# First four pairs' scores from float32 operands on two row halves, zero products at the start, one value block per pair, shared tail products, and an order from a table: a fused attention and gated MLP on one Trainium2 core

## The chip, the cores and the metric

The kernel runs on one core of a Trainium2 chip. The metric is the device time of one execution in microseconds (us), the median of several runs. An engine is named as the profile names it: PE is the matrix engine and PEld its weight loads, DVE the vector engine, ACT the scalar engine, POOL the GpSimd engine, and SP the engine whose queue issues all the DMA transfers of this kernel.

## The reference

For each of 8 batches and 8 heads, 576 queries of 64 numbers meet 576 keys. Scores further than tau below their row's maximum are dropped; the rest go through a softmax and weight the values. The 8 heads of a batch, side by side, are then the input of a gated MLP whose gate mixes along the sequence:

```python
scores = scale * np.matmul(q, k.transpose(0, 1, 3, 2))
thresh = np.max(scores, axis=-1, keepdims=True) - tau
scores = np.where(scores >= thresh, scores, -1000000000.0)
attn = np.exp(scores - np.max(scores, axis=-1, keepdims=True))
attn = attn / (np.sum(attn, axis=-1, keepdims=True) + 1e-09)
x = np.matmul(attn, v)                      # heads side by side: 576 x 512 per batch
h = gelu(x @ w_in)                          # 576 x 1024
u, v = h[..., :512], h[..., 512:]
v_n = layernorm(v) * g_ln
v_s = w_sg @ v_n + b_sg[:, None]            # along the sequence
out = x + (u * v_s) @ w_out
```

## The kernel before

**Pairs and tiles.** Work is cut into 32 *pairs*, two heads of one batch each (`attention(n, ...)`, n = 0 to 31), and 8 batches of the MLP (`moe(b, ...)`), each of which needs its four pairs. A head's 576 queries are four tiles of 128 and a tail of 64; the tails of the two heads share one tile, so a pair has 9 score tiles of 128 x 576. For each tile, PE makes the scores (`scores`, L750), DVE takes the row maximum (`maxima`, L759), POOL the threshold (L765), ACT the exponential (L785), DVE drops what lies below the threshold and sums (`select`, L792), PE transposes the tile in 128 x 128 pieces (`turn`, L516; 45 per pair with those of the inverse sums) and ACT copies the result out (L870, L889). Then PE multiplies by the values (`values`, L900), DVE multiplies by the inverse sums (`finish`, L912), and ACT and POOL split the result `x` into a high part `xh` and a rest `xl` (L916, L920).

**Split operands.** A product with full precision is made from operands that are split into a high part and a rest in the format fp32r: high times high, high times rest, rest times high, three products of one pass each. `products` (L980) issues those of the MLP. Plain float32 operands need no split, but the array takes several passes; the profile shows such a product as two records. For the scores of a pair, one operand `qst` stacks the high part and the rest of q over the 128 rows, `ks` holds the high part of k twice, and `klz` the rest of k beside zeros, so two products give a score half of 288 columns; the shared tail tile takes four. Placing q and k for this needs ACT (L665), POOL (L669, L692) and ten DMAs of a pair (L676, L684, L698). Only pair 0 (`WHOLE_SCORES = 1`) uses plain float32 operands `rk`, `rq` of 64 rows each, with no splitting and placing.

**Value blocks.** `values` is called twice per pair, for 256 and for 320 queries (`PARTS`), each a block of 10 products of plain float32, 64 columns of the array per head, two heads beside each other: 20 records.

**The MLP of a batch** has five v units (four of 128 rows, one of the 64 tail rows, 512 columns, 12 products each: L1037 to L1074 normalise them), then u, gate and down units (L1114, L1128, L1132, L1157, L1160). Its weights arrive as doubles and are turned into split float32 by `from_double`: 16 jobs, five steps on DVE each (L553 to L567), two on ACT (L547, L548) and the splitting (L568, L569).

**The order.** The kernel is first recorded by a `Planner`, which gives every step a place (`Step.time` plus an offset per kind, `OFF`, and per group, `START`), prices each operation (`time_of`), and lists the steps in the order in which its engines would take them: among the steps ready within `LOOK[engine]` of the soonest, the one with the lowest place. PE's eight banks are handed out in the same walk. The real program is then written in this one order, and each engine and the SP queue run their instructions in it, one after the other.

## Time and profile before

| | |
|---|---|
| times of the runs shown (us) | 1030.94, 1033.41, 1036.24; median 1033.41 |
| the profiled execution: span (us) | 1032.0, 1.4 below the median and within the runs |
| instructions in the trace | 20160 |
| mean granted clock of PE | 0.995 |

The profile's span runs from the first to the last instruction; the time of a run has been within 4.2 of it in all three. Views of the profile used below: the busy table by engine, the stretches (busy time and number of instructions of each engine between two times), the groups of instructions by line, the chain of work that ended last, the timeline, the waits, and the DMA issues. In a group's row, `x` is the count, then come the busy time and the mean of one in ns, then the engine's idle time just before them. In a row of the chain or the timeline the first number is the start, the second the length, both in us.

### The profile page before, as it was taken

What the parts mean: (1) busy time and instruction counts of PE and PEld (TensorE: products, weight loads), DVE (VectorE), ACT (ScalarE), POOL (GpSimd) and SP (SyncE); (2) the same over time, 40 slices, a digit from 0 to 9 for tenths busy, and PEclk for the clock granted to TensorE, in tenths of its full rate; (3) what the DMA queues carried; (4) which work ended last, traced back from release to release, by engine and by line L of the source; (5) the groups of instructions that cost most, each with busy time, mean ns of one, the idle gap of its engine ahead of it and who ended that gap; (6) DMA issues with size and microseconds to landing.
All of it is one profiled execution on the core that took longest, in us unless ns stands there. A gap on an engine that the chain in (4) does not pass through costs nothing.

```text
span 1032.0 us, 20160 instructions
## 1 busy us (share of the span) xinstructions
PE 985.4 (95%) x6972; PEld 839.1 (81%) x6972; DVE 664.5 (64%) x1431; ACT 696.3 (67%) x1501; POOL 606.4 (59%) x1085
## 2 busy tenths in 40 slices
PE   4988989999999999999999999999999999999997
PEld 2666767898779987799788988799878997889887
DVE  3888998573776647855586647766477564773350
ACT  4788788674786658856687657766578665875362
POOL 5575668655565475554656565554746646644566
PEclk9999999999999999999999999999999999999999
DMA  8575353343242434324143342424334242300001
GB/s 248 136 202 129 91 137 84 91 117 104 60 112 60 110 100 110 97 78 106 58 108 87 108 114 69 103 54 115 101 86 108 64 113 65 98 21 22 21 7 47
DMA packets 51336, 96.43 MB, mean 93 GB/s; under 512 B 8097, under 2 KB 16289, under 8 KB 51234
## 3 DMA queue, kind: packets, MB, share of 16 engines
q1 hardware_dynamic: 51234, 95.15, 34.7%
q8 instruction: 55, 0.90, 0.4%
q14 instruction: 47, 0.39, 0.1%
HBM read 38.44 MB, written 9.44 MB: 46 GB/s over the span
## 4 chain that ended last, share of the span: by engine, by line
PE 59%; DMA 10%; POOL 9%; ACT 8%; DVE 7%; issue 6%; SPq 1%; POOLq 0%; DVEq 0%; ACTq 0%
PE all_banks L980 26%; PE all_banks L750 12%; PE all_banks L900 11%; PE all_banks L516 10%; DMA qst<-qhi 4%; DVE p L792 3%; ACT pt L870 2%; POOL ot L1160 2%; DMA qst<-rq 2%; DMA ks<-khi 1%; ACT p L785 1%; DMA w<-in_w_in 1%; DVE nm L759 1%; POOL rk L669 1%; POOL vv L1059 1%
## 5 line engine op out<-in xcount | busy, mean ns | idle before, releaser
L792 DVE SCALAR_TENSOR_TENSOR p<-all_banks,nm,p 128x576 f32<-128x576 f32 x256 | 204.6, 812 | 96.3 <-ACT p L785 51.0
L759 DVE TENSOR_REDUCE nm<-all_banks 128x1 f32<-128x576 f32 x288 | 212.3, 751 | 69.4 <-PE all_banks L750 65.3
L785 ACT ACTIVATE p<-all_banks,nm 128x576 f32<-128x576 f32 x256 | 187.3, 747 | 51.1 <-DVE nm L759 49.3
L750 PE MATMUL all_banks<-ks,qst 128*128 128x288 f32 x620 | 186.6, 319 | 7.2 <-DVE p L792 3.5
L516 PE MATMUL all_banks<-ident_r,p 128*128 128x128 f32 x1152 | 168.2, 282 | 15.5 <-DVE p L792 12.9
L870 ACT ACTIVATE pt<-all_banks 128x512 f32<-128x512 f32 (+1 forms) x320 | 165.4, 556 | 13.6 <-PE all_banks L516 12.4
L750 PE MATMUL all_banks<-klz,qst 128*128 128x288 f32 x620 | 172.5, 296 | 0.2
L516 PEld LDWEIGHTS all_banks<-ident_r,p 128*128 128x128 f32 x1152 | 135.7, 145 | 37.8 <-DVE p L792 15.9
L750 PEld LDWEIGHTS all_banks<-ks,qst 128*128 128x128 f32 x620 | 117.7, 190 | 30.9 <-DVE p L792 14.6
L900 PE MATMUL all_banks<-pt,rv 128*64 128x320 f32 (+1 forms) x1024 | 138.3, 412 | 1.7 <-ACT ir L832 1.5
L750 PEld LDWEIGHTS all_banks<-klz,qst 128*128 128x128 f32 x620 | 118.0, 190 | 2.1 <-DMA klz<-rk 0.6
L765 POOL TENSOR_TENSOR nm<-columns,nm 128x1 f32<-128x1 f32 x288 | 57.7, 207 | 99.6 <-DVE nm L759 76.0
L980 PE MATMUL all_banks<-wsh,z 128*128 128x288 f32 (+2 forms) x512 | 112.7, 296 | 1.5 <-DVE uu L963 0.6
L900 PEld LDWEIGHTS all_banks<-pt,rv 128*64 128x64 f32 x1024 | 67.8, 136 | 50.9 <-issue 8.8
L980 PEld LDWEIGHTS all_banks<-wsh,z 128*128 128x128 f32 x512 | 85.4, 188 | 2.8 <-DVE uu L963 0.9
L1132 POOL TENSOR_TENSOR gl<-uu,gh 128x288 fp32r<-128x288 f32 (+2 forms) x64 | 51.3, 804 | 54.7 <-ACT gh L1128 54.6
L980 PE MATMUL all_banks<-xh,wih 128*128 128x288 f32 (+2 forms) x256 | 78.4, 306 | 0.0
L980 PE MATMUL all_banks<-xh,wil 128*128 128x288 f32 (+2 forms) x256 | 76.5, 299 | 0.0
L980 PE MATMUL all_banks<-gh,woh 128*128 128x288 f32 (+2 forms) x256 | 76.3, 299 | 0.1
L980 PE MATMUL all_banks<-gl,woh 128*128 128x288 f32 (+2 forms) x256 | 75.5, 296 | 0.6 <-POOL gl L1132 0.5
L980 PE MATMUL all_banks<-xl,wih 128*128 128x288 f32 (+2 forms) x256 | 75.4, 295 | 0.0
L980 PE MATMUL all_banks<-wsl,z 128*128 128x288 f32 (+2 forms) x256 | 75.4, 294 | 0.0
(114 smaller groups left out, 2192.7 us busy)
## 6 DMA issues: line engine op xcount, KB each, us to landing
rk<-in_kT SPq DMA_DIRECT2D x32, 320.0 KB, 3.2
rv<-in_vP SPq DMA_DIRECT2D x32, 320.0 KB, 3.1
ks<-khi SPq DMA_DIRECT2D x62, 160.0 KB, 2.6
rq<-in_qT SPq DMA_DIRECT2D x32, 288.0 KB, 3.1
qst<-rq SPq DMA_DIRECT2D x62, 144.0 KB, 3.1
qst<-qhi SPq DMA_DIRECT2D x62, 144.0 KB, 3.4
ks<-khi SPq DMA_DIRECT2D x62, 144.0 KB, 2.5
out_T<-ot SPq DMA_DIRECT2D x56, 144.0 KB, 1.8
```

Of the source, the lines that this page charges most:

```text
L516: nc.tensor.transpose(out, x, ident_r.bitcast(F32))
L669: nc.gpsimd.tensor_tensor(st["k"].bitcast(F32R), st["k"], st["kh"], ALU.subtract)
L750: nc.tensor.matmul(sc[:, a, 0:HALF], w, x, start=(j == 0), stop=(j == len(terms) - 1))
L759: nc.vector.tensor_reduce(nmax, st["s", h, i][:, :, 0:HALF], AX.XY, ALU.max, negate=True)
L765: nc.gpsimd.tensor_tensor(thr, toff, st["nm", h, i], ALU.subtract)
L785: nc.scalar.activation(target(h, i), st["s", h, i][:, :, 0:HALF], AF.Exp, bias=st["nm", h, i])
L792: nc.vector.scalar_tensor_tensor(dst, st["s", h, i][:, :, 0:HALF], st["thr", h, i], dst, ALU.is_ge, ALU.mult, accum_out=st["l", p][:, c:c ...
L870: nc.scalar.activation(dst, src, AF.Copy)
L900: nc.tensor.matmul(acc[h * D:(h + 1) * D, 0:w], st["v"][:, o:o + D], unit(h, p)[:, kt, 0:w] if kt < NM else tail_unit(p)[:, 0:w], start=(k ...
L980: nc.tensor.matmul(st["acc"], *term(j), start=(j == 0), stop=(j == n - 1))
L1132: nc.gpsimd.tensor_tensor(st["gl", p, d], st["u", p, d], st["gh", p, d], ALU.subtract)
L1160: return lambda: nc.gpsimd.tensor_tensor(o(), o(), x[b, m][:, ts_], ALU.add)
```

## The change

1. **Scores of pairs 0 to 3** come from float32 operands (`WHOLE_SCORES = 4`). `half_scores` issues one product per half and head, and the two heads' products, in the upper and the lower 64 rows of the array, follow each other. The shared tail tile is made on row halves and column halves at once. Pairs 0 to 3 need no splitting or placing of q and k, and their q and k are loaded at the start into eight separate places.
2. **Scores of pairs 4 to 31**: the rest of k (`kl`) is used where POOL writes it, against the high part of q beside zeros (`qz`, two DMAs per pair, one set for all pairs); the tail tile takes three products instead of four, with `qd`, a diagonal of the two tails (two small DMAs). `klz` and its DMAs are gone.
3. **One value block per pair** (40 records in two banks), and with it one guard, reciprocal, inverse, multiply and split per pair; the last pair keeps two.
4. **Shared tail products**: the tail of `xl` is also written behind `xh` (one POOL instruction per pair), so the v unit of the tail makes 8 products of 128 rows instead of 12 of 64; ACT copies the upper half out and DVE adds it.
5. **Zero products**: six float32 products of 256 columns on the zeroed `pm` are the first thing PE does. The zeroing of constants moves from POOL to DVE.
6. **Order**: each step's place comes from a table of numbers (packed in `PLACES`) in place of `OFF` and `START`; `LOOK` and the planner's prices are other numbers, and it counts a price of 165 ns where PE's products change between the whole array and halves of it.

```diff
-OFF = dict(
-    tau=18.0, q_tails=18.88, w_load=-20.35, w_abs=-36.92, w_word=1.51, w_mul=108.69, w_add=115.91, w_hi=-17.64,
...
+PLACES = (
+    "c-nPX2Rv2p|G($jWbctZvq!clg>2FiDMTd^iS)A)Q8biNW|7h&Eg~{Pp|UrTJ+jyB-gEx$IQO3G`})6J=id9A=RD76z2Berb5Rh4LT$WIge&0%"
...
-LOOK = dict(tensor=124.5, vector=56.7, scalar=75.9, gpsimd=57.5, sync=1079.7)
-WHOLE_SCORES = 1
+LOOK = dict(tensor=71.71, vector=187.35, scalar=179.86, gpsimd=257.13, sync=1209.65)
+WHOLE_SCORES = 4
+WARM = 6
...
-        self.place = [0.0] + [s.time + s.scale * OFF[s.kind] + START.get(s.group, 0.0) for s in plan]
+        table = np.frombuffer(zlib.decompress(base64.b85decode(PLACES)), np.uint8).astype(np.uint16).reshape(2, -1)
+        places = np.cumsum((table[0] * 256 + table[1]).astype(np.int16).astype(int))
...
+        def f(k):
+            x = bank(f"warm{k}")
+            nc.tensor.matmul(x[:, 0:2 * P], pm[:, 0:P], pm[:, 0:2 * P], start=True, stop=True)
...
+        parts = SPLIT if n == B * HP - 1 else ((0, S),)
...
-            nc.gpsimd.tensor_tensor(st["k"].bitcast(F32R), st["k"], st["kh"], ALU.subtract)
+            st["kl"] = kpool.tile([P, KW], F32R, tag="kl", name=f"kl{n}")
+            nc.gpsimd.tensor_tensor(st["kl"], st["k"], st["kh"], ALU.subtract)
...
-        def k_place_lo(h):
-            def f():
-                rows, (w, o) = slice(h * D, (h + 1) * D), (KW, 0) if h else (S, TAIL)
-                st["kl", h] = klz[h][n % 2]
-                nc.sync.dma_start(st["kl", h][rows].bitcast(F32), st["k"][rows, o:o + w])
-            return f
+        def q_place_alone():
+            for h in range(2):
+                rows = slice(h * D, (h + 1) * D)
+                nc.sync.dma_start(qz[h][rows].bitcast(F32), st["qh"][rows, :S].bitcast(F32))
...
+                rows, o, lo = slice(h * D, (h + 1) * D), i * P, a * HALF + (1 - h) * TAIL
+                qo = o + h * TAIL
+                nc.tensor.matmul(st["s", h, i][:, a, 0:HALF], st["q"][rows, qo:qo + P], st["k"][rows, lo:lo + HALF],
+                                 start=True, stop=True)
...
-                    elif i < NM:
-                        terms = [(q[h][:, qo:qo + P], k[:, ko:ko + HALF]) for k in (st["ks", h], st["kl", h])]
+                    if i < NM:
+                        terms = [(q[h][:, qo:qo + P], st["ks", h][:, ko:ko + HALF]),
+                                 (qz[h][:, qo - h * TAIL:qo - h * TAIL + P], st["kl"][:, lo:lo + HALF])]
                     else:
-                        terms = [(w, k[:, ko + g * TAIL:ko + g * TAIL + HALF])
-                                 for g, w in enumerate((q[0][:, MAIN:KW], q[1][:, 0:P]))
-                                 for k in (st["ks", g], st["kl", g])]
+                        terms = [(w, st["ks", g][:, ko + g * TAIL:ko + g * TAIL + HALF])
+                                 for g, w in enumerate((q[0][:, MAIN:KW], q[1][:, 0:P]))]
+                        terms.append((qd[n % 2], st["kl"][:, TAIL + ko:TAIL + ko + HALF]))
...
+                for a, (c0, w) in enumerate(got):
+                    for kt in range(NM + 1):
+                        for h in range(2):
+                            o, cs = kt * P + h * D, slice(c0, c0 + w)
+                            nc.tensor.matmul(st["acc", p][h * D:(h + 1) * D, a, 0:w], st["v"][:, o:o + D],
+                                             unit(h)[:, kt, cs] if kt < NM else tail_unit()[:, cs],
+                                             start=(kt == 0), stop=(kt == NM))
...
+                c, k = divmod(j, 2)
+                return xh_of[b, c][:, ts_], (wih, wil)[k][c][:, FH:DF]
...
-            acc = products(put, time, spread, f"v{b}_{i}", (rows, FH), term, 3 * NC)
+            acc = products(put, time, spread, f"v{b}_{i}", (P, FH), term, (3 if i < NM else 2) * NC)
...
+        for k in range(WARM):
+            at("warm", 0.0, partial(f, k))
```

What the table and the new code do to the order is seen at two places. The first is DVE around the multiply of pair 3 (`x32_3` before, `ir3` now), after which the products of batch 0 can begin; `w` and `room` are steps of the weight jobs, `nm` and `p` those of score tiles. Before:

```order
L963 SCALAR_TENSOR_TENSOR vv0_1_1274<-gt0_1_1231,all_banks_91 128x512
L559 TENSOR_SCALAR room6_807<-w6_744 128x512
L1037 BN_STATS bn0_1_1296<-vv0_1_1274 128x6
L792 SCALAR_TENSOR_TENSOR p4_0_1213,l4_0_1214<-all_banks_91,nm4_1_0_1251,p4_0_1213 128x576
L1040 BN_AGGR bn0_1_1296<-bn0_1_1296 128x2
L759 TENSOR_REDUCE nm4_1_1_1311<-all_banks_91 128x1
L792 SCALAR_TENSOR_TENSOR p4_1_1288,l4_0_1214<-all_banks_91,nm4_0_1_1266,p4_1_1288 128x576
L912 TENSOR_TENSOR x32_3_1_1331<-all_banks_91,ir3_1_1268 128x320
L792 SCALAR_TENSOR_TENSOR p4_1_1288,l4_0_1214<-all_banks_91,nm4_1_1_1311,p4_1_1288 128x576
L553 TENSOR_SCALAR room14_1318<-room14_1318 128x256
L555 TENSOR_SCALAR room7_832<-room7_832 128x512
```

And now:

```order
L668 TENSOR_TENSOR w18_944<-w18_944 128x256
L654 TENSOR_SCALAR room19_969<-room19_969 128x256
L656 TENSOR_SCALAR room19_969<-room19_969 128x256
L658 SCALAR_TENSOR_TENSOR w19_932<-w19_932,room19_969 128x256
L668 TENSOR_TENSOR w20_1037<-w20_1037 128x256
L902 SCALAR_TENSOR_TENSOR p4_0_1138,l4_1139<-all_banks_91,nm4_0_0_1133,p4_0_1138 128x576
L660 TENSOR_SCALAR room19_969<-w19_932 128x256
L1037 TENSOR_TENSOR ir3_1090<-all_banks_91,ir3_1090 128x576
L870 TENSOR_REDUCE nm4_1_0_1165<-all_banks_91 128x1
L668 TENSOR_TENSOR w19_932<-w19_932 128x256
L870 TENSOR_REDUCE nm4_0_1_1177<-all_banks_91 128x1
```

Before, 53 of the 80 DVE steps of the weight jobs stand ahead of this multiply, with some of pair 4 and two early v units of batch 0; now 79 of the 80 do, with one tile of pair 4 and nothing of the MLP.

The second place is PE in the v unit of the tail of batch 0 (`wih`, `wil` are the split halves of w_in, `xh`, `xl` those of x, by pair). Before, 12 products for 64 rows:

```order
L980 MATMUL all_banks_91<-wih0_104,xh0_470 64x512
L980 MATMUL all_banks_91<-wil0_108,xh0_470 64x512
L980 MATMUL all_banks_91<-wih0_104,xl0_484 64x512
L980 MATMUL all_banks_91<-wih1_105,xh1_646 64x512
L980 MATMUL all_banks_91<-wil1_109,xh1_646 64x512
L980 MATMUL all_banks_91<-wih1_105,xl1_673 64x512
L980 MATMUL all_banks_91<-wih2_106,xh2_938 64x512
L980 MATMUL all_banks_91<-wil2_110,xh2_938 64x512
L980 MATMUL all_banks_91<-wih2_106,xl2_983 64x512
L980 MATMUL all_banks_91<-wih3_107,xh3_1177 64x512
L980 MATMUL all_banks_91<-wil3_111,xh3_1177 64x512
L980 MATMUL all_banks_91<-wih3_107,xl3_1203 64x512
```

And now 8 for 128 rows, the row of the first one included:

```order
L1113 MATMUL all_banks_91<-wih0_104,xh0_475 128x512
L1113 MATMUL all_banks_91<-wil0_108,xh0_475 128x512
L1113 MATMUL all_banks_91<-wih1_105,xh1_705 128x512
L1113 MATMUL all_banks_91<-wil1_109,xh1_705 128x512
L1113 MATMUL all_banks_91<-wih2_106,xh2_946 128x512
L1113 MATMUL all_banks_91<-wil2_110,xh2_946 128x512
L1113 MATMUL all_banks_91<-wih3_107,xh3_1167 128x512
L1113 MATMUL all_banks_91<-wil3_111,xh3_1167 128x512
```

The four products with `xl` are gone, since its tail now stands in the second half of the 128 columns of `xh`.

Elsewhere in the order: of the pairs 4 to 31, the last product that reads `kl` and `qz` of one pair and the first of the next lie apart by other PE work, between pairs 10 and 11 by 51 products of 288 columns, 18 transposes and one short product; between the others by 0.9 to 1.4 times as much, each row counted at one price per kind. On SP, `tau`, which scales q, is the fifth DMA now and was the sixth.

363 lines of the change are left out of this document (249 added, 114 removed), and 10 rows, old and new, of the table START.

## The prediction, on record before the result was known

> **What bounds the kernel now.** I read the busy table first, then the stretches, then the chain and the groups inside the stretches that are not full.
>
> ```profile
> PE 985.4 (95%) x6972; PEld 839.1 (81%) x6972; DVE 664.5 (64%) x1431; ACT 696.3 (67%) x1501; POOL 606.4 (59%) x1085
> ```
>
> PE is busy 95% of the span and no other engine over 67%. An average hides stages, so I cut the span. In a row of the stretches come the length, then the busy time and instruction count of PE, PEld, DVE, ACT and POOL, PE's granted clock, the DMA share and GB/s:
>
> ```profile
> 0.00:20.00 20.00, 7.54 (x20) 4.41 (x20) 4.47 (x13) 6.87 (x11) 12.86 (x28) 1.00 0.81 262
> 20.00:120.00 100.00, 89.35 (x535) 65.79 (x536) 89.30 (x189) 79.02 (x171) 63.06 (x106) 0.98 0.59 153
> 120.00:160.00 40.00, 32.02 (x223) 25.21 (x222) 38.19 (x80) 32.58 (x71) 26.40 (x47) 0.96 0.44 118
> 160.00:1010.00 850.00, 840.53 (x6087) 727.97 (x6086) 530.69 (x1148) 573.40 (x1241) 490.00 (x888) 1.00 0.31 82
> 1010.00:1032.00 22.00, 16.00 (x114) 15.74 (x112) 1.90 (x4) 4.41 (x10) 14.08 (x18) 0.93 0.16 55
> ```
>
> From 160 to 1010 us PE is busy 840.5 of 850 with 7.2 records per us: there a product less is time less. Before that the record counts fall to 5.4 per us (20 to 120), while DVE is busy 89% and then 95%: the start is DVE's. "Busy" flatters PE there too, because it ran slowly at first. Pieces of the chain, start and length in us:
>
> ```profile
> 25.73 2.21 PE all_banks L750 x4
> ...
> 30.33 1.33 PE all_banks L516 x5
> ...
> 93.43 2.84 PE all_banks L900 x20
> ...
> 102.68 2.38 PE all_banks L900 x20
> ...
> 147.28 0.98 PE all_banks L516 x9
> ...
> 159.23 2.76 PE all_banks L980 x12
> ...
> 168.40 1.57 PE all_banks L750 x12
> ```
>
> Transposes took 266 ns each at 30 us and 109 ns at 147: half rate first. At full rate a product of 288 columns takes 131 ns, one of 512 takes 230 ns, and the two value blocks 2.84 + 2.38 = 5.22 us. So a pair costs PE 40 x 0.131 + 45 x 0.109 + 5.22 = 15.4 us.
>
> **Part 1, products that go away (full stretch).** Shared tail of the scores: 6 products instead of 8 (two halves) in 28 pairs, 28 x 2 x 0.131 = **7.3 us**. Tail v unit: 8 instead of 12 in 8 batches, 8 x 4 x 0.230 = **7.4 us**. That the 8 fill 128 columns of the array and not 64 costs nothing: by their groups, both widths take the same.
>
> ```profile
> L980 PE MATMUL all_banks<-wih,xh 128*128 128x512 f32 x128 | 51.8, 405 | 0.6 <-ACT xh L916 0.4 <-ACT pt L870 0.2
> L980 PE MATMUL all_banks<-wih,xh 128*64 128x512 f32 x32 | 13.1, 408 | 0.0
> ```
>
> One value block for two: a block is ten pairs of records; a column costs 2 x 0.109/256 = 0.85 ns per pair of records by the transposes (two passes of 128 columns), so 256 columns need 2.18 us and 320 need 2.72, and the blocks took 0.20 and 0.12 more. That is the price of going into and out of a block, at least 0.12; I take 0.20, since a transpose's 109 ns holds some overhead of its own, and 27 pairs lose one block each: **5.4 us** (3.2 to 6). What is added there lies beside PE: a POOL copy of 64 columns per pair, per batch an ACT copy and a DVE add of 64 x 512, two small DMAs per pair; from 160 to 1010 POOL, ACT and DVE are idle 42%, 33% and 38%. Without that cover it would cost about 1 us per batch. Merging also takes away one multiply, one split and one guard per pair, all idle-time work. Sum of the full stretch: 20.1 us, between 17.9 and 20.7.
>
> **Part 2, the start.** By 160 us PE had done this much; x is the count of records:
>
> ```profile
> L516 PE MATMUL all_banks<-ident_r,p 128*128 128x128 f32 x216 | 37.1, 310 | 14.1 <-DVE p L792 12.0 <-DVE nm L759 1.2 <-ACT tt L889 0.5
> L750 PE MATMUL all_banks<-ks,qst 128*128 128x288 f32 x106 | 35.0, 346 | 3.5 <-ACT pt L870 2.3 <-DVE p L792 1.3
> L750 PE MATMUL all_banks<-klz,qst 128*128 128x288 f32 x106 | 30.5, 304 | 0.0
> L900 PE MATMUL all_banks<-pt,rv 128*64 128x256 f32 (+1 forms) x176 | 23.6, 410 | 1.7 <-ACT ir L832 1.5 <-ACT pt L870 0.2
> L980 PE MATMUL all_banks<-wih,xh 128*128 128x512 f32 x10 | 4.1, 411 | 0.2 <-ACT pt L870 0.2
> ```
>
> 216/36 = 6 pairs of transposes (29.4), 212 score products (27.8) and pair 0's float32 ones (5, below), 176/32 = 5.5 pairs of value blocks (28.7), and about 29 products of v units (three groups like the last, 6.7): 97.6 us at full rate. PE stood 62.4 us behind its own rate, and from there it is full.
>
> In the new order batch 0 starts only after pair 3's multiply, with 79 of the 80 DVE steps of the weight jobs ahead of it. So the start ends at a time T at which PE has done four pairs and two tiles, about 62.5 us: a float32 half beside the other head's costs a value block's 288 columns, 2.61/10 = 0.26 us for two heads, so 20 such are 5.2 us per pair, as before. The start is T - 62.5 behind, even with before at T = 125. DVE's work up to T, from a tile's two steps and the weight groups:
>
> ```profile
> 14.13 0.82 DVE L792 SCALAR_TENSOR_TENSOR p<-all_banks,nm,p 128x576 f32<-128x576 f32 x1 [1.06 <-ACT p L785]
> ...
> 14.87 1.42 DVE L759 TENSOR_REDUCE nm<-all_banks 128x1 f32<-128x576 f32 x2
> ```
>
> ```profile
> L557 DVE SCALAR_TENSOR_TENSOR w<-w,room 128x512 uint32<-128x512 uint32 (+1 forms) x16 | 11.4, 720 | 0.0
> L567 DVE TENSOR_TENSOR w<-w 128x512 f32<-128x512 f32 (+1 forms) x16 | 11.0, 700 | 0.0
> L553 DVE TENSOR_SCALAR room<-room 128x512 f32<-128x512 f32 (+1 forms) x16 | 9.7, 613 | 2.6 <-ACT room L547 2.6
> L559 DVE TENSOR_SCALAR room<-w 128x512 uint32<-128x512 uint32 (+1 forms) x16 | 8.9, 563 | 0.0
> L555 DVE TENSOR_SCALAR room<-room 128x512 uint32<-128x512 uint32 (+1 forms) x16 | 6.3, 401 | 0.0
> L630 DVE TENSOR_TENSOR bias_lo<-w,bias_hi 1x576 fp32r<-1x576 f32 x1 | 2.0, 1959 | 0.3 <-ACT bias_hi L626 0.3
> ```
>
> A tile is 14.87 - 14.13 = 0.74 plus 0.71, 36 tiles 52.2 us. The weights are 49.3, less an overlap with the neighbour of about 0.06 each (an 0.82 step gives way after 0.74), 44.5. Multiplies and reciprocals, about 3. Of these 99.7, 4.5 were done by 20 us before and I take the same now: 95.2 left. At the pace of 120 to 160 (95%) T = 120; without a gap 115; at that of 20 to 120 (89%) 127. I take 120, so the start gains **5 us** (between 10 and -2), because DVE's gaps of before lay partly behind what pairs 1 to 3 no longer have:
>
> ```profile
> 58.58 2.84 DMA klz<-rk
> ...
> 62.42 4.63 DMA qst<-qhi
> ...
> 106.37 3.81 DMA qst<-qhi
> ```
>
> The weight price can be lower still. The same step takes 0.42 us alone and 1.73 us beside a POOL step:
>
> ```profile
> 23.65 0.42 DVE L559 TENSOR_SCALAR room<-w 128x512 uint32<-128x512 uint32 x1
> ...
> 48.75 1.54 POOL L669 TENSOR_TENSOR rk<-rk,khi 128x640 fp32r<-128x640 f32 x1 [0.70 <-DMA qst<-rq]
> ...
> 48.85 1.73 DVE L559 TENSOR_SCALAR room<-w 128x512 uint32<-128x512 uint32 x1
> ```
>
> The POOL splits of pairs 1 to 3 (six steps) are gone; if each had held DVE for 1.3 us, that is up to 8 us, which I leave to a rival. The zero products lie in a wait that PE has anyway; the first scores still wait for q's scale:
>
> ```profile
> PE all_banks L750 <- POOL rq L688: 10.0, 1, 10.0
> ```
>
> The x4 at 25.73 are two float32 products of 288 columns at half rate, 1.1 us each; six of 256 are then 6 x 1.1 x 256/288 = 5.9 us, and end near 8 us; if they overran, pair 0 would start that much later. Zeroing on DVE falls into its idle time before `columns`. `tau` is issued one DMA earlier, but q of pair 3 is scaled ahead of pair 0's: nothing either way (within 0.8 us).
>
> **Part 3, the order in the full stretch.** PE's idle time there, 9.5 us, is the most a better order can give back; a worse one could add as much. I take 0.
>
> **Sum.** 1032.0 - 20.1 - 5 = 1006.9 for the span, and with the 1.4 by which the median stands above it, **1008 us**.
>
> **The rivals.** *A slow array in the start.* Before, PE stayed at half rate through pair 0 although busy:
>
> ```profile
> 20.00:43.00 23.00, 21.70 (x67) 15.05 (x68) 20.41 (x40) 15.82 (x33) 11.65 (x18) 1.00 0.63 162
> ```
>
> If the zero products do not help and four pairs of float32 and transposes leave it so, or if the two heads' products do not overlap, PE needs up to 2 x 61.4 us from 10 us on, T = 133, and the start loses 8 instead of gaining 5: 1021. Against it: value blocks of 40 records come without a break, and the block quoted at 93 us ran at full rate in such a mix. Chance 0.10. The Trainium skill, TensorE: Matmul & The Clock Gate, Part 1, says that the array doubles its rate after about 3.4 us of sustained work and falls back after an idle window as long; Part 4 says that transposes do not count as busy. The half rate above fits the first, the slow 23 us fit the second, and by both the zero products' effect may be lost before the scores come, as this rival has it.
>
> *The start gains more.* DVE without a gap and weights 8 us cheaper: T = 107, 18 us gained, 995. Chance 0.10.
>
> *Slower: one set of `qz` and `kl`.* Between two pairs, POOL and SP must wait for the last product that reads the old set; what stands behind in SP's queue (placing of `ks`, the next loads) waits with it, and the next pair's scores for both. From the DMA issues, median us to landing last, over the whole span and over the first 40 us:
>
> ```profile
> qst<-qhi SPq DMA_DIRECT2D x62, 144.0 KB, 3.4
> ```
>
> ```profile
> qst<-rq SPq DMA_DIRECT2D x2, 144.0 KB, 10.7
> ```
>
> Two issues of 0.5 and a landing of 3.4 make 4.4 us; the order puts 51 x 0.131 + 18 x 0.109 = 8.6 us of other PE work there. It decides from a chain of 9.8 us on (27 gaps of 1.2 eat 31 us: slower than before); at the 10.7 of the crowded start it would be 11.7, 27 x 3.1 = 84 us lost, 1092. Against it: the DMA share is 0.31 here, not 0.7. Chance 0.05.
>
> *The order gives back the gain:* the waits of PE in the full stretch grow from 9.5 us to two or four times that and pay away 10 to 28 us: 1018 to 1036. Chance 0.09; nothing in the trace speaks for it but that every place in the table is new.
>
> **How the numbers follow.** The forecast, all products gone and the start between -2 and 10, has 0.66. The range 996 to 1024 takes its bounds (20.7 + 10 gained, 17.9 - 2 gained, some us of order to each side) and the slow array, and leaves out parts of the second, third and fourth rival. What a measurement can tell here is about 0.5%, 5 us: faster (below 1028) has 0.66 + 0.10 + 0.10 and a third of the fourth, in all 0.89; the rest of the fourth is no change; so same 0.06, and slower 0.05.
>
> **What would show it.** Right: from about 160 us on still over 7 records per us and PE about 99% busy, value blocks of 40 records in about 5.0 us, the multiply of pair 3 near 120 us, DVE over 90% busy until then. Wrong: PE waiting at the first `kl` or `qz` product of a pair; transposes at 213 ns or more after 50 us; the multiply of pair 3 past 130 us.

## The result, and the profile after

The changed kernel took 1041.22 us (median of 4 runs, 1037.89 to 1042.16) against 1032.18 for the kernel before beside it: 1.0072 times as long, 95% interval 1.0047 to 1.0096. It is slower by 0.7%, where the prediction had 1008 us, a range of 996 to 1024, and 5 in 100 for slower. The profiled execution took 1042.16 us with a span of 1040.4. In the table of experiments below, one of the four runs of e4 was slow (1054.62 us): it counts in the median and not in the ratio.

The stretches of the changed kernel (length, then busy time and instruction count of PE, PEld, DVE, ACT and POOL, PE's granted clock, DMA share, GB/s):

```profile
0.00:20.00 20.00, 14.34 (x40) 10.47 (x41) 9.30 (x29) 4.84 (x7) 4.44 (x14) 0.76 0.89 320
20.00:120.00 100.00, 82.28 (x375) 50.94 (x373) 79.80 (x144) 63.11 (x128) 56.06 (x74) 0.74 0.32 90
120.00:160.00 40.00, 34.92 (x186) 24.36 (x187) 31.73 (x67) 25.44 (x55) 17.66 (x37) 0.87 0.08 23
160.00:1010.00 850.00, 833.83 (x6124) 733.74 (x6123) 551.68 (x1143) 593.16 (x1235) 490.15 (x856) 1.00 0.34 88
1010.00:1040.40 30.40, 24.76 (x182) 24.23 (x180) 3.38 (x8) 8.63 (x19) 22.20 (x28) 0.96 0.11 40
```

The full stretch is nearly as full as it was: 7.2 records per us, with PE busy 833.8 of 850 us, so that it stands idle for 16.2 us where it did for 9.5. The start is not: from 20 to 120 us PE now handles 375 records instead of 535, at a granted clock of 0.74. The 0.98 of before in that row is too high. The trace of before has no record of the clock until 42.65 us, and a stretch without a record counts as full, while its transposes took 266 ns each at 30 us, half rate; with half rate from 20 to 42.65 us the row would have 0.87. The 1.00 in the prediction's row from 20 to 43 us has the same reason. DVE, which was to be busy 95%, is busy 79.8%. The multiplies that end pairs 0 to 3, as one group (durations min/median/max in ns, then the first and the last start in us):

```profile
L1037 DVE TENSOR_TENSOR ir<-all_banks,ir x4: 744/751/758, 54.5 to 146.3; 128x576 f32<-128x576 f32 x4
```

The last one is the prediction's T: 146.3 us, where it had 120. Pieces of the chain, start and length in us:

```profile
57.85 2.21 PE all_banks L836 x4
...
110.62 1.23 PE all_banks L836 x4
111.86 5.00 PE all_banks L1024 x40
116.86 1.18 PE all_banks L836 x8
...
126.81 1.26 PE all_banks L607 x5
```

The value block of 40 records takes 5.00 us, as forecast. The score products (L836, two records each) are the surprise. Two products of one head take 1.23 us at full rate and 2.21 at half; four, two of one head and then two of the other, take 1.18. They share the array only when the two heads' products stand right behind each other, and in the new order they mostly do not: each half product is a step of its own in the table, and over pairs 0 to 3 they come as LLLLHHHH, LL, HHHH, LL, LLLHHL, HH and so on (L is the head in rows 0 to 63, H the other), with transposes between the groups. The last row shows transposes at half rate far into the start. What all this costs PE and DVE by T, by groups (count, busy us, mean ns, and the idle time before them with what ended it); first PE to 160 us, then DVE to 146.3:

```profile
L836 PE MATMUL all_banks<-rk,rq 64*128 64x288 f32 x128 | 44.6, 532 | 10.0 <-POOL rq L791 3.9 <-ACT pt L989 3.7 <-DVE p L902 2.4
L607 PE MATMUL all_banks<-ident_r,p 128*128 128x128 f32 x166 | 35.3, 360 | 10.4 <-DVE p L902 10.4
...
L850 PE MATMUL all_banks<-rk,rq 64*64 64x288 f32 x32 | 7.7, 623 | 0.0
```

```profile
L870 DVE TENSOR_REDUCE nm<-all_banks 128x1 f32<-128x576 f32 x37 | 27.6, 753 | 24.0 <-PE all_banks L836 17.6 <-PE all_banks L850 4.1 <-issue 1.5
...
L658 DVE SCALAR_TENSOR_TENSOR w<-w,room 128x512 uint32<-128x512 uint32 (+1 forms) x16 | 18.4, 1148 | 0.3
```

The four pairs' scores take PE 44.6 + 7.7 = 52.3 us; the sum had 5.2 a pair, 20.8. DVE stands idle 24.0 us in front of its maxima, 21.7 of it waiting for those products, and PE's transposes wait 10.4 us for DVE's `p`. The sum had 5 us of idle time for DVE in all. From 20 us to T, first the changed kernel, then f4, in which those products are short and on full rows (see below):

```profile
20.00:146.31 126.31, 105.25 (x491) 64.99 (x490) 100.17 (x189) 78.55 (x163) 67.05 (x96) 0.75 0.27 76
```

```profile
20.00:130.77 110.77, 79.32 (x492) 51.77 (x491) 100.43 (x192) 78.08 (x165) 67.81 (x98) 0.86 0.30 87
```

DVE's work there is 100.2 us in one and 100.4 in the other; its idle time is 26.1 and 10.3.

### The profile page after: what moved, and what is told of

Its sections match the earlier page's. It is cut to its first block, busy times and chain, and to the rows that moved or that the text cites. A ratio compares the mean times of both kernels' runs of the same rounds, so it can differ in the third digit from the quotient of the medians.

```text
span 1040.4 us, 19810 instructions
## 1 busy us (share of the span) xinstructions
PE 990.1 (95%) x6900; PEld 843.7 (81%) x6900; DVE 675.9 (65%) x1389; ACT 695.2 (67%) x1441; POOL 590.5 (57%) x1006
## 4 chain that ended last, share of the span: by engine, by line
PE 68%; POOL 8%; ACT 8%; DVE 8%; issue 4%; DMA 3%; SPq 1%; POOLq 0%; ACTq 0%; DVEq 0%
PE all_banks L1113 30%; PE all_banks L607 13%; PE all_banks L861 10%; PE all_banks L1024 10%; PE all_banks L836 3%; DVE p L902 2%; DVE nm L870 2%; ACT pt L989 1%; DMA ks<-khi 1%; ACT p L895 1%; POOL vv L1208 1%; POOL z L1221 1%; ACT vv L1205 1%; POOL bn L1197 1%; DVE vv L1096 1%
## 5 line engine op out<-in xcount | busy, mean ns | idle before, releaser
L989 ACT ACTIVATE pt<-all_banks 128x512 f32<-128x512 f32 (+1 forms) x320 | 172.8, 555 | 64.7 <-PE all_banks L607 59.5
L607 PE MATMUL all_banks<-ident_r,p 128*128 128x128 f32 x1152 | 184.2, 286 | 18.1 <-DVE p L902 17.5
L607 PEld LDWEIGHTS all_banks<-ident_r,p 128*128 128x128 f32 x1152 | 142.4, 147 | 42.7 <-DVE p L902 23.0
L861 PE MATMUL all_banks<-ks,qst 128*128 128x288 f32 x560 | 158.9, 315 | 7.3 <-DVE p L902 2.8
L1024 PE MATMUL all_banks<-pt,rv 128*64 128x288 f32 (+2 forms) x1024 | 140.2, 417 | 0.0
L861 PE MATMUL all_banks<-kl,qz 128*128 128x288 f32 x448 | 124.7, 295 | 0.0
L861 PEld LDWEIGHTS all_banks<-ks,qst 128*128 128x128 f32 x560 | 102.1, 188 | 22.5 <-issue 6.4
L861 PEld LDWEIGHTS all_banks<-kl,qz 128*128 128x128 f32 x448 | 84.5, 189 | 0.5
L1037 DVE TENSOR_TENSOR ir<-all_banks,ir 128x576 f32<-128x576 f32 (+2 forms) x33 | 24.2, 734 | 81.6 <-PE all_banks L1024 69.4
L1113 PE MATMUL all_banks<-gh,woh 128*128 128x288 f32 (+1 forms) x240 | 72.6, 303 | 0.4 <-ACT tt L1004 0.4
## 6 DMA issues: line engine op xcount, KB each, us to landing
qz<-qhi SPq DMA_DIRECT2D x56, 144.0 KB, 2.4
qst<-qhi SPq DMA_DIRECT2D x56, 144.0 KB, 2.5
ks<-khi SPq DMA_DIRECT2D x56, 144.0 KB, 2.6
qst<-rq SPq DMA_DIRECT2D x56, 144.0 KB, 2.6
```

Source lines behind the costliest of these rows:

```text
L607: nc.tensor.transpose(out, x, ident_r.bitcast(F32))
L861: nc.tensor.matmul(sc[:, a, 0:HALF], w, x, start=(j == 0), stop=(j == len(terms) - 1))
L989: nc.scalar.activation(dst, src, AF.Copy)
L1024: nc.tensor.matmul(st["acc", p][h * D:(h + 1) * D, a, 0:w], st["v"][:, o:o + D], unit(h)[:, kt, cs] if kt < NM else tail_unit()[:, cs], st ...
L1037: nc.vector.tensor_tensor(x, st["acc", p][:, :, 0:w // m], x, ALU.mult)
L1113: nc.tensor.matmul(st["acc"], *term(j), start=(j == 0), stop=(j == n - 1))
```

## The experiments

Eighteen kernels ran. "T" is the multiply of pair 3, "clock" the granted clock from 20 to 120 us. Ratios are to the kernel before, run on the same chip, whose median was 1029.9 to 1033.8 us. e6 and g4 have no clock here: their traces record none until 39.5 and 31.7 us. Of each edit, the lines that carry it are shown, and `...` marks lines left out between them.

| run | median us | ratio, 95% interval | T | clock |
|---|---|---|---|---|
| changed kernel | 1041.22 | 1.0072 (1.0047-1.0096) | 146.3 | 0.74 |
| e1 heads together | 1032.46 | 1.0013 (0.9995-1.0032) | 137.8 | 0.79 |
| e2 full rows | 1043.81 | 1.0119 (1.0085-1.0152) | 149.9 | 0.85 |
| e3 16 zero products | 1062.37 | 1.0307 (1.0264-1.0349) | 167.3 | 0.65 |
| e4 fewer weight steps | 1044.23 | 1.0101 (1.0052-1.0149) | 147.8 | 0.76 |
| e5 one float32 pair | 1107.15 | 1.0703 (1.0663-1.0743) | 149.2 | 0.74 |
| e6 before, four pairs | 1042.33 | 1.0085 (1.0055-1.0114) | | |
| e7 together, fewer weight steps | 1035.07 | 1.0018 (0.9995-1.0040) | 139.1 | 0.77 |
| e8 together, 16 zero products | 1043.25 | 1.0085 (1.0053-1.0117) | 144.0 | 0.73 |
| f1 half time, order kept | 1027.52 | 0.9956 (0.9939-0.9972) | 132.9 | 0.73 |
| f2 full rows, order kept | 1031.94 | 1.0004 (0.9990-1.0019) | 138.9 | 0.86 |
| f3 fewer weight steps, order kept | 1025.70 | 0.9953 (0.9934-0.9971) | 133.7 | 0.82 |
| f4 = f1 and f2 | 1025.23 | 0.9938 (0.9920-0.9956) | 130.8 | 0.86 |
| g1 weights later | 1049.15 | 1.0186 (1.0150-1.0223) | 139.6 | 0.78 |
| g2 = g1 and f2 | 1043.78 | 1.0135 (1.0110-1.0159) | 133.4 | 0.90 |
| g3 = f4 and f3 | 1018.70 | 0.9891 (0.9866-0.9916) | 122.3 | 0.88 |
| g4 before, fewer products | 1026.10 | 0.9945 (0.9922-0.9968) | | |
| h1 other order, measured price | 1029.27 | 0.9984 (0.9961-1.0006) | 139.7 | 0.67 |
| h2 other order, the table's price | 1018.40 | 0.9895 (0.9863-0.9927) | 124.6 | 0.81 |

### First eight: one part at a time, the order made anew

The first theory: score products of one head alone cost twice the price and hold the rate down, so PE bounds the start. The rival: the order of the table, with nearly all weight steps ahead of pair 3's multiply, bounds it through DVE.

e1, the four half products of a tile pair issued together (`take` is how many places of the table a step uses up; it stands at the earliest, or with 0 at that of the step ahead of it):

```diff
-                for a in range(2):
-                    for hh in (h, 1 - h):
-                        at("s", g, half_scores(hh, i, a))
+                at("s", g, half_scores(h, i, 0), take=4)
+                at("s", g, together(h, i), take=0)
```

> The changed kernel, but the four half products of a tile pair (two heads, two column halves) are issued together, one head's rows and the other's in turn, at the earliest of their four places in the table. Theory (the products of one head's 64 rows stand alone in the new order, so they take twice the array's time and do little for its rate; TensorE bounds the start): a pair's sixteen products fall from about 7.7 to 4.2 us at full rate and from 15.4 to 8.4 at half, so four pairs save 14 us or more; the multiply of pair 3 comes at 125 to 132 us instead of 146, and the time is 1020 to 1028 us against 1041. Rival 1 (the start is set by the table's order and the weight steps on VectorE): the multiply stays at 142 or later, 1037 to 1042. Rival 2 (the clock alone: the overlap saves array time but the array still runs at half rate for 70 of the first 133 us): 1030 to 1036.

T fell to 137.8 and the time to 1032.46: less than the theory, in the range of rival 2. DVE is full now from 20 to 120 us (96.0), at a clock of 0.79:

```profile
20.00:120.00 100.00, 73.84 (x391) 44.21 (x388) 95.98 (x172) 67.93 (x144) 66.39 (x90) 0.79 0.32 96
```

e2, rows filled with zeros (by two more DMAs per pair), and e3, more zero products:

```diff
+                nc.sync.dma_start(q[h][rows, h * TAIL:h * TAIL + S].bitcast(F32), st["q"][rows, :S])
...
-                nc.tensor.matmul(st["s", h, i][:, a, 0:HALF], st["q"][rows, qo:qo + P], st["k"][rows, lo:lo + HALF],
+                nc.tensor.matmul(st["s", h, i][:, a, 0:HALF], q[h][:, o:o + P].bitcast(F32), st["k"][:, lo:lo + HALF],
```

> The changed kernel, but each float32 score product of the first four pairs runs over all 128 rows: q of one head in its 64 rows and zeros in the other 64, against both heads' k. The order is the table's; each product still takes 288 columns' time by itself and no two can overlap. Two more DMAs per pair place q. Theory (rate part: half a row's worth of work does not hold the array's full rate): the stretches at half rate after 30 us nearly go, the multiply of pair 3 comes at 120 to 130 us, and the time is 1018 to 1028 us against 1041. If rows do not matter for the rate: half-rate stretches of 60 to 75 us as in the changed kernel, and 1041 to 1046 us, since the first scores come 3 to 4 us later. Rival 1 (VectorE and the table set the start): rate up, but the time within 5 us of 1041.

```diff
-WARM = 6
+WARM = 16
```

> The changed kernel with 16 products on zeros at the start instead of 6, so that they reach the first scores. Theory: the array enters pair 0 at full rate and keeps it to about 20 us, after which it falls as before: 2 to 6 us gained, 1035 to 1039 us against 1041. Rival 3 (the whole loss of the start is that the zero products end 4 us too early, and a rate once reached would hold): the half-rate stretches go, and 15 us or more are gained, 1026 or less. No effect (1041) if the rate falls in the first window of half-row products.

e2 gave 1043.81, no gain, though the clock rose to 0.85; its first scores came some 8 us later. e3 gave 1062.37, 21 us slower than the changed kernel, which nothing on the list foresaw.

e4, three of four bit steps of each weight left out:

```diff
-        for step in range(4):
-            put("w_word", time + 0.08 * step, lambda step=step: word(step))
+        put("w_word", time, lambda: word(3), take=4)
```

> The changed kernel without three of the four VectorE bit steps of each of the 16 weight pieces (their output is therefore not the reference's); this takes about 27 us of VectorE's work out of the first 150 us. Theory (TensorE bounds the start): VectorE had gaps of about 20 per cent anyway; the multiply of pair 3 comes at most 8 us earlier, 1033 to 1041 us. Rival 1 (the weight steps that the table puts ahead of pair 3's multiply hold the start): the multiply comes 20 us earlier or more, 1015 to 1021 us.

1044.23, T 147.8: taken alone this says that DVE's work costs nothing. That reading turned out wrong (f3).

e5, float32 scores in pair 0 only:

```diff
-WHOLE_SCORES = 4
+WHOLE_SCORES = 1
```

> The changed kernel with float32 scores on row halves in pair 0 alone: pairs 1 to 3 take their scores from three products with split operands as the later pairs do; the table's order is kept, their added steps standing at the place of q's scale and of k's load. Theory (float32 products of one head's rows by themselves slow the start): the start is near that of before, the multiply of pair 3 at 118 to 130 us, what the rest gained (17 us) shows, and the time is 1013 to 1023 us. Rival 1 (the table's order of the start, whatever the products): 1035 us or more. Rival 4 (both are good for half): 1025 to 1032.

T stayed at 149.2 with the three-product scores, and behind it batches took up to 143 us instead of 118: 1107.15. This speaks against the first theory as it stood.

e6, the four pairs in the kernel before, under its own rules:

```diff
-WHOLE_SCORES = 1
+WHOLE_SCORES = 4
...
```

> The kernel before with one thing of the change: the scores of the first four pairs from float32 operands on row halves (its rules set the order, and there too one head's two products stand by themselves). Theory: the start grows as it did in the changed kernel, by 10 to 25 us: 1040 to 1055 us against 1031. Rival 1 (the table is the cause, the four pairs are not): within 5 us of 1031, or faster, since three pairs' splits and placements are gone.

1042.33, ratio 1.0085. In that order too the four pairs cost about 9 us; PE is as busy from 20 to 120 us as before (89.4) with 66 records fewer (its 0.98 is too high, as that of before is):

```profile
20.00:120.00 100.00, 90.64 (x469) 58.51 (x468) 90.50 (x192) 72.87 (x160) 61.66 (x108) 0.98 0.26 76
```

e7 is e1 with e4's edit, e8 is e1 with e3's:

> The products of the two heads together (as in the first of these runs) and three of four VectorE bit steps of the weights left out (output not the reference's). With the products together VectorE was busy 99 per cent from 20 to 80 us. Theory (array first, VectorE next): now the weight steps are worth something, 10 us or more: 1012 to 1022 us against 1032. If the clock and the chain of one pair set the start even then: 1027 to 1032.

> The products of the two heads together and 16 products on zeros at the start. 16 products on zeros alone made the changed kernel 21 us slower, with the array at half rate for 95 us of the first 159. Theory (at half rate the products of one head alone fill the time and keep the rate down, so where it falls is a matter of chance; together they are too short for that): 1026 to 1035 us against 1032. If zero products harm in themselves (16 of them are 4 us late or take a bank from the scores): 1045 or more.

1035.07 and 1043.25, where e1 had 1032.46: neither edit helps there.

What follows: little. In all of these the planner made a new order (from the same table, or in e6 from the same rules), because an edit changed the steps or their prices, and a new order can move T by as much as the edit: f3 below is e4's edit in the old order. So the next runs hold the order.

### f1 to f4, g3: the order kept row for row

The planner works on the changed kernel as it is; only what a step then issues differs. f1 (two one-pass products on the upper halves of the numbers), f2 (128 rows, q with zeros in the other head's rows) and f3:

```diff
+                upper = [st[x].bitcast(mybir.dt.bfloat16).rearrange("p (c w) -> p c w", w=2)[rows, :, 1] for x in "qk"]
+                for j in range(2):
+                    nc.tensor.matmul(st["s", h, i][:, a, 0:HALF], upper[0][:, qo:qo + P], upper[1][:, lo:lo + HALF],
+                                     start=(j == 0), stop=(j == 1))
```

```diff
+                    nc.tensor.matmul(st["s", h, i][:, a, 0:HALF], wide[n % 2][h][:, o:o + P], st["k"][:, lo:lo + HALF],
+                                     start=True, stop=True)
```

```diff
+            if planned and step < 3:
+                return
```

In f2, f4, g2 and g3 one wide q serves two pairs and is written for the second of them (pair 2 over pair 0, pair 1 over pair 3) before the first has read it all, so most products of pairs 0 and 3 run on the wrong pair's q. The shapes of the products are unchanged; pair 0's third product waits 0.86 us for it in f2.

> The changed kernel with its order of instructions kept, row for row (the runs so far let the planner place the steps anew). Each float32 score product of one head in the first four pairs is replaced by two one-pass products on the upper halves of the same numbers (bfloat16), so the output is not the reference's; a product then takes about 0.25 us at full rate instead of 0.5, what the prediction took it for. Theory 1 (the products' own time, because they stand alone): the multiply of pair 3 comes at 122 to 132 us instead of 146, and the time is 1017 to 1027 us. Theory 2 (in this order each pair's steps wait for one another, whatever TensorE's time for the scores): 138 us or later, 1033 or more.

> The changed kernel with its order kept; each float32 score product of the first four pairs runs over 128 rows (q in the head's 64 rows, zeros in the others, made by two more ScalarE steps per pair), so it takes the same time and only the rate can change. Theory 1, its rate part (products on half the rows count half for the rate): half-rate stretches fall from 72 us to 30 or less, the multiply of pair 3 comes at 125 to 135 us, 1020 to 1030 us. If the rate follows idle time and not rows: 60 to 75 us at half rate and 1038 to 1043. Theory 2: the rate rises but the multiply comes at 140 or later.

> The changed kernel with its order kept, without three of the four VectorE bit steps of each of the 16 weight pieces (output not the reference's): 27 us less of VectorE's work in the first 150 us. Rival 1 (VectorE bounds the start, as the prediction had it): the multiply of pair 3 at 125 us or earlier, 1020 or less. Theories 1 and 2: at 140 or later, 1034 or more.

> The two edits together, order kept: score products of the first four pairs over 128 rows and in half the time (output not the reference's). That is what the prediction took these products for: short, and full work for the rate. Theory 1: the multiply of pair 3 at 115 to 125 us, the time 1010 to 1020, which would close the sum. Theory 2: 135 us or later, 1030 or more.

> The changed kernel's order, with score products of the first four pairs over 128 rows and in half the time, and without three of the four bit steps of each weight piece (output not the reference's). With all three terms of the prediction's start made smaller than it took them, what is left is the order itself: if the terms are all, the multiply of pair 3 comes at 105 to 118 us (VectorE has about 83 us of work left) and the time is 998 to 1012. If a pair's steps wait for one another in any case: 120 or later, 1013 or more.

T in f1, f2, f3, f4 and g3, in this order (pair 0's start, then pair 3's):

```profile
L1044 DVE TENSOR_TENSOR ir<-all_banks,ir x4: 744/752/758, 50.2 to 132.9; 128x576 f32<-128x576 f32 x4
```

```profile
L1047 DVE TENSOR_TENSOR ir<-all_banks,ir x4: 745/753/758, 55.3 to 138.9; 128x576 f32<-128x576 f32 x4
```

```profile
L1040 DVE TENSOR_TENSOR ir<-all_banks,ir x4: 747/758/758, 49.5 to 133.7; 128x576 f32<-128x576 f32 x4
```

```profile
L1050 DVE TENSOR_TENSOR ir<-all_banks,ir x4: 748/758/758, 52.9 to 130.8; 128x576 f32<-128x576 f32 x4
```

```profile
L1052 DVE TENSOR_TENSOR ir<-all_banks,ir x4: 746/757/758, 47.9 to 122.3; 128x576 f32<-128x576 f32 x4
```

Behind T nothing changes: span less T is 894.1 us in the changed kernel and 893.2, 893.1, 893.2, 892.4 and 892.9 in these (spans 1026.1, 1032.0, 1026.9, 1023.2, 1015.2). So T carries the whole difference, and the parts can be read off. Products in half the time: 13.4 us. Rows alone: 7.4. Both: 15.5, less than their sum. The three bit steps, which take DVE's busy time by T from 109.5 to 81.0 us: 12.6. All three: 24.0. The stretches from 20 to 120 us of f1, f2 and f4 show which part is which:

```profile
20.00:120.00 100.00, 74.24 (x402) 44.49 (x398) 85.75 (x157) 68.26 (x140) 59.74 (x83) 0.73 0.33 96
```

```profile
20.00:120.00 100.00, 75.36 (x391) 50.45 (x392) 83.50 (x155) 65.49 (x136) 58.36 (x78) 0.86 0.32 93
```

```profile
20.00:120.00 100.00, 69.77 (x431) 45.54 (x429) 91.03 (x169) 72.42 (x150) 60.36 (x86) 0.86 0.33 96
```

f1 is quicker at the same clock (0.73 for 0.74). f2 has as many products as the changed kernel, in the same order and with the same count of columns, and its clock is 0.86. What differs in them is the other 64 rows, zeros against the other head's k, so these raised it (f2 also scales q once more on ACT, which makes the first scores no earlier: 11.5 us for 11.0). With both, DVE comes to 91% busy, near the prediction's 95%, but T is 130.8 and not 120. DVE's idle time in front of its maxima from 20 us to T falls from 19.9 us to 2.9:

```profile
L870 DVE TENSOR_REDUCE nm<-all_banks 128x1 f32<-128x576 f32 x33 | 24.7, 753 | 19.9 <-PE all_banks L836 13.4 <-PE all_banks L850 4.1 <-issue 1.5
```

```profile
L883 DVE TENSOR_REDUCE nm<-all_banks 128x1 f32<-128x576 f32 x34 | 25.1, 751 | 2.9 <-PE all_banks L849 2.6 <-PE all_banks L874 0.3
```

e4 and f3 are one edit, with T 147.8 in a new order and 133.7 in the old. e2 and f2 differ in how q is placed as well, but there too T is later with a new order (149.9 and 138.9) at nearly the same clock.

### g1, g2: can the weights simply go later?

The eight pieces of w_out, moved behind T, one step after every four others:

```diff
+    at = [p for p, i in enumerate(rest) if plan[i].kind == "rmul"][3] + 1
...
+    for i in sorted(moved, key=lambda i: (moved[i], i)):
+        out += [i, *rest[at:at + EVERY]]
...
```

> The changed kernel with its order kept but for one thing: the steps of the eight pieces of w_out (first used by batch 0's last products, far behind) are moved from before to behind the multiply of pair 3, one after every four other steps; the output is the reference's. That takes about 22 us of VectorE's work out of the time before that multiply. Leaving out 27 us of such work moved the multiply by 12.6 us. Theory (TensorE and VectorE take turns in the start, so either one's work counts for about half): the multiply comes at 134 to 139 us instead of 146, and since VectorE is idle a third of the time behind it, 1029 to 1035 us against 1041. If the moved steps hold pair 4 and batch 0 instead: 1036 or more.

> The weights of w_out moved as in the run before, and the float32 score products of the first four pairs over 128 rows (q with zeros in the other head's rows, scaled by VectorE, two short steps per pair). Rows alone moved the multiply of pair 3 by 7.4 us. If the two gains add: the multiply at 126 to 132 us and 1021 to 1028 us, faster than both kernels. If they overlap, as halving the products and filling the rows did (13.4 and 7.4 alone, 15.5 together): 1027 to 1033.

T came to 139.6, and the time went up to 1049.15. From 140 to 200 us, first the changed kernel, then g1:

```profile
140.00:200.00 60.00, 54.77 (x376) 43.94 (x376) 47.54 (x97) 45.71 (x94) 35.68 (x65) 1.00 0.24 59
```

```profile
140.00:200.00 60.00, 45.82 (x287) 36.76 (x287) 53.65 (x112) 44.33 (x94) 36.95 (x64) 0.97 0.26 70
```

DVE is 6 us busier there and PE does 89 records fewer: the moved steps stand ahead of pair 4's and batch 0's on DVE. In g1 span less T is 908.1, 14 us more than in the others. Moved in this way, they cost more behind T than they save ahead of it. The edit also gives the moved pieces two other buffers (those of `xl6` and `xh6`); what that adds was not tried by itself. g2 loses the same way (133.4 and 1043.78).

### g4: the prices of the full stretch

```diff
+                    if planned and n > 3 and i == NM:
+                        terms = terms[:3]
...
+                m = 8 if planned and shape[0] < P else n
```

> The kernel before, its order kept, with the products left out that the change saves in the full stretch apart from the value blocks: 4 of the 12 of each batch's tail v unit, and 2 of the 8 tail score products of pairs 4 to 31 (output not the reference's). The prediction's price: 32 x 0.230 + 56 x 0.131 = 14.7 us, 1016 to 1018 against 1031. If other engines' waits fill part of the room: 1019 to 1025.

The period of a batch is the cleanest reading: the last multiply of pair 7 and of pair 27, five batches apart, in before, g4 and the changed kernel:

```profile
254.22 0.47 DVE L912 TENSOR_TENSOR x<-all_banks,ir 128x320 f32<-128x320 f32 x1
...
859.61 0.47 DVE L912 TENSOR_TENSOR x<-all_banks,ir 128x320 f32<-128x320 f32 x1
```

```profile
248.59 0.47 DVE L915 TENSOR_TENSOR x<-all_banks,ir 128x320 f32<-128x320 f32 x1
...
845.59 0.47 DVE L915 TENSOR_TENSOR x<-all_banks,ir 128x320 f32<-128x320 f32 x1
```

```profile
259.07 0.76 DVE L1037 TENSOR_TENSOR ir<-all_banks,ir 128x576 f32<-128x576 f32 x1 [7.38 <-POOL rq L795]
...
851.48 0.76 DVE L1037 TENSOR_TENSOR ir<-all_banks,ir 128x576 f32<-128x576 f32 x1 [8.14 <-PE all_banks L1024]
```

A batch takes 121.1 us in before, 119.4 in g4 and 118.5 in the changed kernel. The two products' price by the prediction is 8 x 0.131 + 4 x 0.230 = 1.97 us a batch, measured 1.7; with four blocks of 0.20 it is 2.77, measured 2.6. All three come from one profiled execution each. The median of g4 shows less than its period: 1026.1, a gain of some 4 to 6 us, where the profiled run (the quickest of ten, 1020.18) has a span 13.6 shorter than before. Why the other nine are slower stays open.

### h1, h2: the same instructions in another order

The first 1099 steps were put in another order by small moves; every instruction is the changed kernel's. h1 was searched at the price that these runs had shown, h2, as the control, at the price that the table was made for.

```diff
+    first = np.frombuffer(zlib.decompress(base64.b85decode(ORDER)), np.uint16).tolist()
...
+    order[:len(first)] = first
```

> The changed kernel with the same instructions (output the reference's) in another order up to about 200 us, and nothing else: the first 1000 steps were put in an order found by many small moves that bring the products of the start to an earlier end, at the prices that these runs showed: a score product of one head by itself takes 0.48 us at full rate and counts half for the rate, two of different heads issued one right behind the other share that time, tau lands at 9.1 us. Theory (the order in the table was made for score products at half the time they take by themselves, and it is this that costs the start; with the right price the same instructions can do it): the multiply of pair 3 at 115 to 130 us instead of 146, 1008 to 1023 us, faster than both kernels. If the four float32 pairs cannot be done faster in any order: 1030 or more.

> The control: the same number of small moves from the same order, but at the price that the table was made for (a score product of one head at half that time, and full work for the rate, wherever it stands). Theory: the moves spoil on the chip what they gain by the wrong price; the multiply of pair 3 at 130 to 145 us, 1024 to 1040 us, at least 10 us behind the run with the right price. If only the amount of searching matters and not the price: within 5 us of the other.

The control won: 1018.40 against 1029.27. h2 is faster than both kernels, by 1.05% than before (interval 0.73 to 1.37). So the idea that the wrong price spoils the order is not borne out by this pair. But the order alone, with the same output, is worth 23 us, and the change is not slower than before by its instructions. The start of h1, then of h2:

```profile
0.00:20.00 20.00, 9.62 (x39) 6.66 (x39) 10.84 (x33) 7.61 (x12) 3.90 (x13) 0.78 0.77 260
20.00:120.00 100.00, 88.28 (x375) 54.70 (x374) 81.16 (x142) 59.38 (x124) 55.15 (x74) 0.67 0.33 93
```

```profile
0.00:20.00 20.00, 15.24 (x65) 9.76 (x66) 16.31 (x45) 13.14 (x22) 10.23 (x20) 1.00 0.59 213
20.00:120.00 100.00, 82.13 (x430) 53.07 (x431) 85.91 (x165) 65.78 (x141) 56.29 (x85) 0.81 0.38 114
```

T was 139.7 and 124.6, span less T 889.9 and 889.8: T decides again. Both issue `tau` first and have their first scores at 5.9 us instead of 11.0. Then h1 falls behind, in these pieces of ACT's and PE's time (in brackets the idle time before, and what ended it):

```profile
13.36 0.66 ACT L699 ACTIVATE room<-w 128x512 f32<-128x512 f32 x1 [3.59 <-DMA w<-in_w_in]
...
14.48 1.35 ACT L946 ACTIVATE p<-all_banks,nm 128x576 f32<-128x576 f32 x2
```

```profile
17.63 1.33 PE L658 MATMUL all_banks<-ident_r,p 128*128 128x128 f32 x5 [6.21 <-DVE p L953]
```

A weight step waits on ACT for its load, the exponentials stand behind it, and PE is idle for 6.2 us. The clock fell to half at 11.4 us and stayed there to 35.3; in h2 it held full to 21.9. From 20 to 120 us h1's clock is 0.67, the lowest but that of e3, and h2's 0.81. By T, DVE has done nearly the same work (107.5 us in h1, 105.4 in h2), while PE was busy 115.3 us in h1 and 102.0 in h2; 11.3 us of that are the four pairs' score products (52.1 and 40.8). So the 15 us between the two go mainly with the array's rate and with what stands beside those products. That the one wait above began it is argued from the trace; it was not tried by itself.

## Why the prediction was wrong, point by point

**Part 1 was right.** A batch became 2.6 us shorter for 2.77 predicted; the value block of 40 records took 5.00 us. Span less T is 894.1 us, where the sum had 1006.9 - 120 = 886.9. So of the 33.5 us by which the span missed, 26.3 lie ahead of T and 7.2 behind it. Of the 7.2 the prices explain 8 x 0.17 = 1.4. The other 5.8 lie outside the five batches measured and stay open. PE's idle time from 160 to 1010 us grew from 9.5 to 16.2 us, 3.5 of it inside the five, where Part 3 took no change; whether the order or the merged blocks made it grow, no run separates.

**Part 2 failed, at the step "a float32 half beside the other head's costs a value block's 288 columns ... so 20 such are 5.2 us per pair".** Beside the other head it does: four products in 1.18 us, two heads' in 0.59 for 0.52 in the sum (its 0.26 is the share of one product; a block's ten are five of each head, so two heads cost twice that). But the order does not put them beside each other, and alone they take twice that, or four times at half rate: 52.3 us for the four pairs instead of 20.8. The order's rows show the products in groups of two and four between transposes, and not whose they are; the sum priced them without asking which head's product stands next.

**The same step hid the rate.** The prediction held that value blocks keep the rate up, and gave a chance of 0.10 to a rival, a slow array or products that do not overlap, at T = 133 and 1021 us. Both of its conditions came true: the clock was 0.74, transposes took 252 ns each at 126.8 us, and T was past 130, two of the three signs of being wrong. PE's work was not too small in it: it had 2 x 61.4 = 122.8 us, and PE was busy 114.1 us between 11 us and T. What it had at nothing is the other 21.2 us of that time, in which PE waits for other engines. Products' time and rate together are 15.5 us of the 26.3 by which T was late (f4).

**T = 120 from DVE's work was the second failure.** The sum had 95.2 us of work and 4.8 of idle time for DVE behind 20 us; there were 100.2 and 26.1. The work was 5 us too small. The rows of the weight steps add up to 52.9 us, where those of before added up to 49.3 (44.5 with the overlap taken off): they became dearer, and not cheaper as the second rival had it, by one step above all (L658, mean 1148 ns, where the same step of before had 720). The idle time was 21 us too small; 17.5 of the 26.1 are the maxima's waits for score products. Where these are short and on full rows (f4), 100.4 us of work and 10.3 of idle time are left, and T is 130.8. The sum also treated DVE as the one bound, with the other engine's work hidden. f1 takes 22.2 us from PE's busy time by T (119.6 to 97.4) and moves T by 13.4; f3 takes 28.5 from DVE's and moves it by 12.6. So about half of what is taken from either comes off. In a start where a pair's maxima wait for PE and its transposes for DVE, neither hides the other.

**The zero products** bought nothing, as the prediction allowed: the clock rose at 7.1 us and fell at 10.6, just as the first scores came at 11.0. **The rival of one set of `qz` and `kl`** did not occur: behind 160 us PE's waits for a DMA of `ks` are 0.5 us in all, and none for `kl` or `qz` is among its waits. **The order** (Part 3, "I take 0") gave nothing in the full stretch, but another one was worth 23 us in the start (h2), where the prediction had counted none of it.

**Luck.** The period of a batch came out within 0.17 us, but in part from two errors that nearly cancel: PE was busy 3.3 us less per batch, not 2.77 (five batches took 599.0 us of its time before and 582.5 now), and stood idle 0.7 us more.

Still open: why a search at the wrong price found the better order; why 16 zero products cost 21 and 11 us (e3, e8), since the order was made anew there; and what the idle time behind T comes from.

## What to carry to other kernels

Price an operation by what stands next to it in the emitted order: an overlap exists only if the order makes it. Where a planner makes the order, keep the order while you test a part; the same edit gave nothing with a new order and 12.6 us of T with a kept one. And where two engines wait for each other in turn, neither one's busy time is the bound: take work from each and see what comes off.

## What the runs showed of the hardware

**Rows count for the rate.** f2 against the changed kernel (0.86 for 0.74) shows it by experiment; one stretch of h1 shows it to the eye, in three windows of 3.41 us, the grid on which the clock changed in every trace:

```profile
28.43:31.84 3.41, 3.35 (x8) 1.93 (x7) 2.90 (x5) 1.44 (x3) 0.77 (x4) 0.50 1.02 231
31.84:35.25 3.41, 3.27 (x16) 3.27 (x17) 3.27 (x7) 3.41 (x8) 2.32 (x3) 0.50 0.16 50
35.25:38.67 3.42, 1.21 (x10) 0.74 (x8) 3.08 (x7) 2.88 (x8) 1.64 (x4) 1.00 0.00 0
```

In the first, PE is busy 3.35 us with 64-row products, and the clock stays at half. In the second it is busy 3.27, 3.15 of it transposes of 128 rows, and in the third the clock is full. From 72.80 to 76.21 us, again at half, 3.30 of 3.41 us are transposes, and the clock is full from 76.22 to 89.86. The Trainium skill, TensorE: Matmul & The Clock Gate, Part 4, says that transposes do not bring the full rate, since they do not count as busy in the same way; these windows say that here they do, and that products on half the rows count for less. The slow 23 us of before, which the prediction laid to transposes, do not speak for that page either: the rate rose at 42.65 us, behind a window with 3.08 of 3.41 us of transposes, and of the 17.9 us that PE was busy from 20 to 39.24 us, 9.1 were products of 64 rows. The third window of h1 shows that PE need not stand still for the rate to fall: it is busy 1.21 of 3.42 us there, and the clock is half behind it.

**A slow array keeps itself slow.** At half rate a lone head's two products fill 2.21 us instead of 1.23, and the first window above, full of them, did not raise the clock; h1 stayed at half rate from 11.4 to 35.3 us, with PE busy 17.6 of the 20 us from 20 to 40. So the more of the time they fill, the less the clock can rise; this is argued from these windows.

**Where a small load stands:** `tau`, issued at 2.6 us behind other loads, landed 6.5 us later; issued first, in h1 and h2, it took 3.1.

```profile
2.58 6.53 DMA columns<-in_tau
```
